# Second-level sums of W_down: one DRAM copy summed in place, and a third set formed on VectorE

## The chip, the cores and the metric

The kernel runs on one core of a Trainium2 chip. The metric is the device time of one execution in microseconds, as the median of several executions. "The profile" is one more execution, recorded by the hardware profiler; its times are counted from the first instruction. TensorE (PE) does the matmuls, VectorE (DVE) and ScalarE (ACT) the element-wise work, GpSimd (POOL) small operations and all DMAs that convert or accumulate, SyncE (SP) issues the other DMAs. All DMAs share 16 DMA engines.

## What is computed

A transformer block on 2048 rows of width D = 1024: layer norm with a modulation from a condition vector, linear attention, and a second half that is a gated MLP with hidden width F = 3584.

```python
h = _layernorm(x) * (1 + ca) + sa
x = x + ga * _A_ref(h, A_wqkv, A_wo)          # linear attention with its projections
h = _layernorm(x) * (1 + cb) + sb
x = x + gb * ((_gelu(h @ w_gate) * (h @ w_up)) @ w_down)
```

Only the last product, with `w_down` (3584 x 1024), is concerned by the change: not the product itself but the preparation of its weights.

## The kernel before

**Products with sums.** Nearly all matrix products are done in Strassen-Winograd form: seven products of half size instead of eight, at the price of sums of blocks of both operands. Some are nested: one of the seven products is itself done in seven. The sums of activations are made on VectorE. Sums of weights are needed too, and for `W_down` they are made ahead of time and kept in DRAM.

**W_down.** Its 28 row blocks of 128 are split into two interleaved halves (`wd_v[0]`, `wd_v[1]`, 14 blocks each), its columns into two halves of 512, which gives four blocks b11, b12, b21, b22. First-level sums t0 to t3 (f16) lie in the DRAM buffer `ts` (`t_scr`): t0 and t2 are made by DMA alone, as a copy that converts from bf16 and then a transfer that accumulates onto it (`wd_todo`, 28 transfers of 256 KB), t1 and t3 on VectorE in `wd_sums` (line 1080): for each of seven pairs of row blocks it loads the raw rows of the second half and the rows of t0, makes two sums and stores them.

Three of the seven products of the down stage are nested (`NESTED`: b21, b22, t0). Each needs second-level sums of its own weight block. With quarters q11, q12, q21, q22 (even or odd row block, left or right 256 columns) these are q11+q12, q11+q12+q22, q12+q22 and q11+q12+q22+q21. They lie in the DRAM buffer `us` (`u_scr`), one slot for each of three blocks and four sums. `second_sums` (line 1064) writes them as chains of DMAs on GpSimd's queue, each of 448 KB in rows of 512 bytes: for every block two copies, an accumulation onto each, a copy of the first sum, an accumulation, a copy of that, an accumulation. That is 24 transfers, 12 copies and 12 accumulations; 8 of the copies are between buffers of the same type or within `us`.

**The order of the work.** All instructions are recorded first and then ordered by a planner (`Plan`). The order on TensorE is the order of recording; on the other engines the planner puts ready instructions by due times, which it finds by sweeping forward and backward over the program with a price for each instruction. A DMA's price is its bytes (`op.bytes`) at 360 GB/s in one serial pipe, plus a latency; an accumulating DMA counts three times its bytes. The result is a fixed order for every engine; at run time an engine waits only for data and for buffers to come free.

`paced_moves` (line 1049) ties a group of DMAs on GpSimd to the progress of the work: a one-element GpSimd copy (L1052) reads a tile that the work has just produced, and the DMAs (issued at L1035) follow it. The 24 transfers are paced so: four after the transformed rows of block 1 (near 48 us), four after those of block 3 (near 117 us), and the other sixteen in the gate/up stage of the first half of the rows: units n = 1 to 4 take two transfers each (second-level sums of b21 and b22), units 5 to 12 one each (those of t0).

**The gate/up stage** (`gate_up`, 248 to 425 us for the first half, 505 to 671 for the second) runs 14 units of some 12 us. Each unit loads 1 MB of `w_gate` or `w_up` (`w_unit`, L1325) into one of three buffers, so that the load of unit n+2 goes out when unit n-1 has ended; VectorE makes the block sums of the next unit's weight (L550, the line of the helper `tt_op`), as fillers between its other work. In the first half, every second unit also runs `wd_sums` for one pair of row blocks and moves two first-level pieces. The norm of the second half of the rows (`late_norm`) also runs here and uses GpSimd for a power (L1204) and for stores (L1208).

**The down stage** (`down_out`, 425 to 505 and 671 to 756 us) reads the sums: `nested` loads seven quarters for each nested product on SP's queue (L1604), four of them second-level sums.

Of the kernel before, what the change touches and what calls it, by code (L numbers as in the profile page):

```python
# [10 lines left out]
FP32 = mybir.dt.float32  # L11
BF16 = mybir.dt.bfloat16
F16 = mybir.dt.float16
AF = mybir.ActivationFunctionType
ALU = mybir.AluOpType
# [8 lines left out]
class Plan:  # L24
# [101 lines left out]
    def aim(self, op):  # L126

        self.ops[-1].early.add(op.n)
        op.late.add(len(self.ops) - 1)

    def cost(self, op, outs, ins):

        size = lambda a: math.prod(d[1] for d in a.ap[1:])
        n = max(size(a) for a in (outs if op.eng == "PE" else outs + ins))
        psum = any(a.tensor.name.startswith("psum") for a in outs + ins)
        wide = any(a.dtype == FP32 and size(a) > 8 for a in outs + ins)
        ptrs = sum(size(a) == 1 for a in ins)
        if op.eng == "PE":
            op.cost = n / 2.4 + 2.5
            op.lat = op.cost + 165  # L140
            if op.fn == "matmul" and outs[0].ap[0][1] <= 32:
                op.cost /= 3.5
        elif op.fn.startswith("dma"):
            a = outs[0]
            op.cost, op.bytes = 1000 if op.eng == "POOL" else 450, math.prod(d[1] for d in a.ap) * (4 if a.dtype == FP32 else 2)
            op.bytes *= 3 if "accum_op" in op.kw else 1
            op.load = a.tensor.name.startswith("mem")
            if op.fn == "dma_start_transpose":
                op.cost, op.bytes = self.transpose
            op.lat = op.cost  # L150
        elif op.eng == "ACT":
            op.cost = (55 if psum else 112) + n / 1.2 + 85 * ptrs
            op.lat = op.cost + 115
            f = op.kw.get("func")
            op.table = "g" if f == AF.Gelu_apprx_tanh else "e" if f in (AF.Exp, AF.Ln) else None
        elif op.eng == "POOL":
            op.cost = 500 if n <= 8 else 250 + n / 0.46
            op.lat = 1800 if n <= 8 else op.cost
        else:
            rate = 1.0  # L160
            if op.fn in ("tensor_scalar", "tensor_scalar_mul", "tensor_scalar_add", "tensor_copy") and not wide:
                rate = 1.0 if psum else 4.0
            elif op.fn == "tensor_tensor" and not wide:
                rate = 2.0
            op.cost = 69 + n / (0.96 * rate) + 61 * ptrs
            op.lat = op.cost + 83
# [119 lines left out]
def kernel(  # L286
# [14 lines left out]
    P = 128  # L301
# [4 lines left out]
    S, D = x_in.shape  # L306
    F = B_w_gate.shape[1]
    KD = D // P
# [6 lines left out]
    NW = min(TG, D)  # L315
# [11 lines left out]
    NPR = JF // 2  # L327
# [4 lines left out]
    mem = mem_pool.tile([P, 103 * KB + KB // 2], BF16, name="mem", tag="mem")  # L332
# [51 lines left out]
    def at(off, shape, dt):  # L384
        return Ring(off, shape, dt, 1)()
# [44 lines left out]
    HB = TG // 2  # L430
# [16 lines left out]
    hr1 = [h12[b // 2][:, b % 2] for b in range(4)]  # L447
# [49 lines left out]
    wdr_ring = Ring(189, [2, D], BF16, 1)  # L497
    wds_ring = Ring(193, [2, 2, NW], F16, 1)
    wds_ring.slots += Ring(183, [2, 2, NW], F16, 1).slots
    wdt_ring = Ring(197, [2, NW], F16, 1)  # L500
    sub_a = [at(76 + 3.5 * j, [NPR // 2, HB], F16) for j in range(3)]
    sub_b = [at(189 + 3.5 * j, [NPR // 2, HB], F16) for j in range(4)]
    x2_ring = Ring(191, [D], BF16, 4)
# [17 lines left out]
    scr_pool = ctx.enter_context(tc.tile_pool(name="scr", bufs=1, space=bass.MemoryType.DRAM))  # L521
# [3 lines left out]
    den_scr = [scr_pool.tile([2, P // DH, 2, KH * TG], BF16, name=f"den{pr}", tag=f"den{pr}") for pr in range(2)]  # L525
    x2_scr = [scr_pool.tile([TG, D], BF16, name=f"x2s{b}", tag=f"x2s{b}") for b in range(NG)]
    t_scr = scr_pool.tile([P, 4, NPR, NW], F16, name="ts", tag="ts")
    u_scr = scr_pool.tile([P, NPR // 2, 3, 4, HB], F16, name="us", tag="us")

    nc.scalar.add_instruction(  # L530
        mybir.InstLoadActFuncSet(name=nc.get_next_instruction_name(), ins=[], outs=[],
# [4 lines left out]
    te, ve, ac, gp, sy = (plan.on(e) for e in ("PE", "DVE", "ACT", "POOL", "SP"))  # L536
# [12 lines left out]
    def tt_op(out, a, b, op):  # L549
        ve.tensor_tensor(out=out, in0=a, in1=b, op=op)  # L550
# [207 lines left out]
    def ln1_block(b):  # L758
        plan.ahead = 4000 if b > 1 else 14000
        for tl in range(TT):  # L760
            xt = load_x(b * TT + tl)
            if b == 1:
                plan.chain.insert((1, 2, 5, 7)[tl], plan.ops[-1])
            mv = ln_stats(xt)
            rstd = pool_rstd(mv)
            nb = nb_ring()
            gp.tensor_scalar(out=nb, in0=mv[:, 0:1], scalar1=rstd, scalar2=-1.0, op0=ALU.mult, op1=ALU.mult)
            xh = xh_ring()
            ac.activation(out=xh, in_=xt, func=AF.Identity, scale=rstd, bias=nb)
            gp.dma_start(out=xa_scr[b][tl * P:(tl + 1) * P, :], in_=xh)  # L770
        sy.dma_start_transpose(out=hr1[b], in_=xa_scr[b][:])
        if b == NG - 1:
            wd_moves(hr1[b][:, 0, 0:1], NPR)
        for kd in range(KD):
            ve.tensor_scalar(out=hr1[b][:, kd, :], in0=hr1[b][:, kd, :], scalar1=opcA[:, kd:kd + 1],
                             scalar2=modT[:, kd:kd + 1], op0=ALU.mult, op1=ALU.add)
        if b != 2:
            paced_moves(hr1[b][:, KD - 1, 0:1], two[b - 1] + two[b])
        plan.ahead = 14000

    def h_sum(b, j):
# [250 lines left out]
    wd_v = B_w_down.rearrange("(i fh p) n -> fh p i n", fh=2, p=P)  # L1032

    def move(dst, src, add):
# [3 lines left out]
    wd_full = {"b11": wd_q[0, 0], "b12": wd_q[0, 1], "b21": wd_q[1, 0], "b22": wd_q[1, 1],  # L1038
               **{f"t{j}": t_scr[:, j] for j in range(4)}}
    NESTED = ("b21", "b22", "t0")  # L1040

    def wd_quarter(name, kh, h):
        return wd_full[name].rearrange("p (i e) n -> e p i n", e=2)[kh][:, :, h * HB:(h + 1) * HB]
# [5 lines left out]
    def paced_moves(seen_of, moves):  # L1049

        plan.hold([op for op in plan.ops if op.eng == "PE"][-1])
        gp.tensor_copy(out=seen, in_=seen_of)  # L1052
        plan.hold(plan.ops[-1])
        for dst, src, add in moves:
            move(dst, src, add)
        plan.hold()
# [4 lines left out]
            paced_moves(seen_of, wd_todo[:n])  # L1061
            del wd_todo[:n]

    def second_sums():


        def chain(x, o):
            q11, q12, q21, q22 = (x[:, :, e, h, :] for e in range(2) for h in range(2))
            o0, o1, o2, o3 = (o[:, :, f, :] for f in range(4))
            return [(o0, q11, 0), (o2, q12, 0), (o0, q12, 1), (o2, q22, 1), (o1, o0, 0), (o1, q22, 1), (o3, o1, 0), (o3, q21, 1)]  # L1070

        raw = wd_v[1].rearrange("p (c e) (j h n) -> p c e j h n", e=2, j=2, h=2)
        t0 = wd_full["t0"].rearrange("p (c e) (h n) -> p c e h n", e=2, h=2)
        b21, b22 = (chain(raw[:, :, :, j], u_scr[:, :, j]) for j in range(2))
        return [[b21[i], b22[i]] for i in range(8)], chain(t0, u_scr[:, :, 2])

    two, t_chain = second_sums()
    late_moves = [two[4], two[5], two[6], two[7], *([m] for m in t_chain)]

    def wd_sums(c):  # L1080


        raw, t, tt = wdr_ring(), wdt_ring(), wds_ring()
        rows = slice(2 * c, 2 * c + 2)
        plan.ahead, plan.extra = 60000, 6000
        sy.dma_start(out=raw, in_=wd_v[1][:, rows, :])
        sy.dma_start(out=t, in_=wd_full["t0"][:, rows, :])
        plan.ahead, plan.extra = 14000, 0

        def last():  # L1090
            tt_op(tt[:, 1], tt[:, 0], raw[:, :, 0:NW], ALU.add)
            for j in range(2):
                gp.dma_start(out=wd_full[f"t{2 * j + 1}"][:, rows, :], in_=tt[:, j])

        return [lambda: tt_op(tt[:, 0], t, raw[:, :, NW:D], ALU.add), last]

    def kvq_phase():

# [301 lines left out]
    def gate_up(g):  # L1400
        h = h2
        rows_inner(g)
        late = late_norm(g + 1) if g + 1 < NGR else []
        w = w_unit(g, 0)
# [19 lines left out]
        inner = None  # L1424
        for n in range(NU):
# [47 lines left out]
            if g == 0 and n % 2 == 0:  # L1473
                fill += wd_sums(n // 2)
                wd_moves(w["s1"][:, 0, 0, 0:1], 2)
            if g == 0 and 1 <= n <= len(late_moves):
                paced_moves(w["s1"][:, 0, 0, 0:1], late_moves[n - 1])
            five = Inner(Y, w["inner"]["t1"], h_inner[g, "t1"]) if "t1" in w["inner"] else None
            if five:
                five.s15()  # L1480
# [28 lines left out]
            inner = None  # L1509
# [23 lines left out]
            w = w_next  # L1533
# [8 lines left out]
    def down_out(g):  # L1542
        NC = 2
        last = g == NGR - 1
# [48 lines left out]
        def nested(name, A, S, keep, out):  # L1593


            j, x = NESTED.index(name), A.rearrange("p (k e) t -> p e k t", e=2)
            at_w = W_AT[g][name]
            dt = F16 if name[0] == "t" else BF16
            y11, y21, y22 = (quarters(at_w[n], [NPR // 2, HB], dt) for n in (0, 1, 6))
            t1, t0, t2, t3 = (quarters(at_w[n], [NPR // 2, HB], F16) for n in (2, 3, 4, 5))  # L1600
            for t, src in ((y11, wd_quarter(name, 0, 0)), (y21, wd_quarter(name, 1, 0)), (t1, u_scr[:, :, j, 1, :]),
                           (t0, u_scr[:, :, j, 0, :]), (t2, u_scr[:, :, j, 2, :]), (t3, u_scr[:, :, j, 3, :]),
                           (y22, wd_quarter(name, 1, 1))):
                sy.dma_start(out=t, in_=src)  # L1604
            x11, x12, x21, x22 = (x[:, e, :, h * HB:(h + 1) * HB] for h in range(2) for e in range(2))
# [123 lines left out]
        def run(*steps):  # L1729
            for f in steps:  # L1730
                f()
# [70 lines left out]
```

## Time and profile before

| | us |
|---|---|
| median of 8 executions | 755.98 |
| lowest and highest | 754.29, 757.92 |
| the profiled execution | 757.47 |
| its span from first to last instruction | 755.7 |
| mean granted clock of TensorE | 0.995 |

The DMA traffic on the two queues, and the transfers that belong to the sums of W_down (line or buffers, engine that issues, number, size of each, median us from issue to landing):

```profile
q1 hardware_dynamic: 128832, 122.44, 53.8%
q0 software_dynamic: 26592, 29.37, 18.2%
...
mem<-us SPq DMA_DIRECT2D x24, 448.0 KB, 8.3
mem<-ts SPq DMA_DIRECT2D x6, 1792.0 KB, 8.5
...
ts<-in_B_w_down_dram POOLq DMA_DIRECT2D x28, 256.0 KB, 8.7
us<-in_B_w_down_dram POOLq DMA_DIRECT2D x12, 448.0 KB, 9.7
```

q1 carries the DMAs of SyncE, q0 those of GpSimd; the columns are packets, MB and the time that the packets took as a share of 16 engines over the span. `mem` is the on-chip memory, `us` and `ts` are the two DRAM buffers. The 12 transfers of the last line are those that read the raw weight; six more go from `us` to `us` and six from `ts` to `us`.

### The profile page before, as it was taken

The page shows a single profiled execution, that of the slowest core. Times are in us where ns is not written, and L with a number is a line of the kernel's source. Part 1 is how long each engine was busy: PE and PEld are TensorE (multiplying, and loading weights), DVE is VectorE, ACT ScalarE, POOL GpSimd, SP SyncE. Part 2 cuts the span into 40 slices and gives each one's busy share as a digit, 9 for nine tenths or more (in the row PEclk, how much of TensorE's full clock was granted, in tenths as well). Part 3 has the DMA queues.
Part 4 walks back from the last instruction along what each step waited for, and adds up shares of the span by engine and source line. Part 5 has one row for each costly group of instructions (what it writes and reads, how often), then busy time and mean ns, then how long its engine had stood idle before and what let it go on. Part 6 is the DMA issues. An engine that isn't in the chain of part 4 may idle for free.

```text
span 755.7 us, 11423 instructions
## 1 busy us (share of the span) xinstructions
PE 731.3 (97%) x4150; PEld 389.4 (52%) x4164; DVE 585.0 (77%) x1230; ACT 432.6 (57%) x757; POOL 120.1 (16%) x183
## 2 busy tenths in 40 slices
PE   5999899999999997999999999999999999999997
PEld 2444445444444443444555486645555555548664
DVE  7897987577775974868797689658788889887763
ACT  3674476669762656989876316017777777641000
POOL 2351257000000240543432000010000000000000
PEclk9999999999999998999999999999999999999999
DMA  9888379939899987998987979952322313399822
GB/s 313 313 179 175 122 172 164 316 137 290 221 295 246 350 184 241 237 319 234 245 228 139 281 227 279 320 182 85 112 75 93 112 57 112 100 273 296 285 99 74
DMA packets 157832, 154.62 MB, mean 205 GB/s; under 512 B 34000, under 2 KB 135888, under 8 KB 156496
## 3 DMA queue, kind: packets, MB, share of 16 engines
q1 hardware_dynamic: 128832, 122.44, 53.8%
q0 software_dynamic: 26592, 29.37, 18.2%
q10 hardware_dynamic: 2352, 2.10, 0.8%
q8 instruction: 32, 0.52, 0.3%
q14 instruction: 24, 0.20, 0.1%
HBM read 127.01 MB, written 37.88 MB: 218 GB/s over the span
## 4 chain that ended last, share of the span: by engine, by line
PE 78%; DMA 9%; DVE 6%; ACT 3%; issue 2%; POOL 1%; SPq 1%; DVEq 0%; ACTq 0%; POOLq 0%
PE psum L1364 30%; PE psum L1570 13%; PE psum L1614 8%; PE psum L1375 7%; PE psum L1244 6%; PE psum L856 5%; PE psum L926 5%; DVE mem L550 4%; DMA mem<-in_B_w_up_dram 2%; DMA mem<-in_B_w_gate_dram 2%; DMA mem<-in_A_wqkv_dram 2%; DMA mem<-in_w_mod_dram 1%; DMA mem<-xas 1%; PE psum L955 1%; DMA xas<-mem 1%
## 5 line engine op out<-in xcount | busy, mean ns | idle before, releaser
L550 DVE TENSOR_TENSOR mem<-mem 128x1024 f16<-128x1024 bf16 (+11 forms) x641 | 303.1, 515 | 41.5 <-ACT mem L801 19.2
L1364 PE MATMUL psum<-mem 128*128 128x512 f16 x1248 | 301.8, 381 | 4.7 <-DVE mem L550 3.1
L801 ACT ACTIVATE mem<-psum 128x256 f32<-128x256 f32 (+3 forms) x284 | 154.3, 562 | 117.4 <-PE psum L1364 42.2
L550 DVE TENSOR_TENSOR mem<-psum,mem 128x512 f16<-128x512 f32 (+4 forms) x204 | 154.8, 766 | 67.0 <-ACT mem L801 21.9
L1364 PEld LDWEIGHTS <-mem 128*128 128x128 f16 (+1 forms) x1248 | 122.7, 98 | 117.4 <-issue 8.8
L1570 PE MATMUL psum<-mem 128*128 128x512 f16 (+2 forms) x458 | 99.0, 372 | 0.7 <-DVE mem L550 0.5
L1375 PE MATMUL psum<-mem 128*128 128x256 f16 x560 | 90.0, 273 | 2.2 <-DVE psum L550 1.9
L1375 PEld LDWEIGHTS <-mem 128*128 128x128 f16 (+1 forms) x560 | 54.9, 98 | 47.9 <-issue 6.3
L1570 PEld LDWEIGHTS <-mem 128*128 128x128 f16 x462 | 45.2, 98 | 49.8 <-issue 0.7
L1614 PE MATMUL psum<-mem 128*128 128x256 f16 (+1 forms) x588 | 66.2, 273 | 0.0
L856 PE MATMUL psum<-mem 128*128 128x512 f16 (+1 forms) x272 | 61.8, 379 | 1.2 <-DVE mem L550 0.8
L1614 PEld LDWEIGHTS <-mem 128*128 128x128 f16 x588 | 57.5, 98 | 9.2
L1418 ACT ACTIVATE psum<-psum 128x512 f32<-128x512 f32 x56 | 32.9, 587 | 44.2 <-PE psum L1364 28.9
L1244 PE MATMUL psum<-mem 128*128 128x512 f16 x256 | 56.0, 379 | 0.0
L926 PE MATMUL psum<-mem 128*128 128x512 f16 x224 | 51.2, 379 | 0.0
L550 DVE TENSOR_TENSOR psum<-psum,mem 128x256 f32<-128x256 f32 x80 | 34.3, 428 | 14.5 <-ACT mem L801 13.8
L856 PEld LDWEIGHTS <-mem 128*128 128x128 f16 x280 | 27.1, 98 | 32.2 <-issue 1.1
L1244 PEld LDWEIGHTS <-mem 128*128 128x128 bf16 x256 | 24.8, 98 | 30.4 <-issue 0.4
L1435 ACT ACTIVATE mem<-psum 128x512 f16<-128x512 f32 x56 | 33.0, 595 | 10.2 <-PE psum L1364 10.1
L1445 ACT ACTIVATE mem<-mem 128x512 f16<-128x512 f16 x56 | 34.1, 625 | 5.3 <-DVE mem L550 5.0
L926 PEld LDWEIGHTS <-mem 128*128 128x128 f16 (+1 forms) x224 | 21.6, 98 | 27.0 <-issue 2.0
L1035 POOL DMA_DIRECT2D ts<-in_B_w_down_dram x28 | 35.3, 1614 | 0.8 <-DMA ts<-in_B_w_down_dram 0.7
(132 smaller groups left out, 556.0 us busy)
## 6 DMA issues: line engine op xcount, KB each, us to landing
mem<-in_B_w_gate_dram SPq DMA_DIRECT2D x14, 1024.0 KB, 9.3
mem<-in_B_w_up_dram SPq DMA_DIRECT2D x14, 1024.0 KB, 7.5
mem<-in_w_mod_dram SPq DMA_DIRECT2D x24, 512.0 KB, 8.6
mem<-us SPq DMA_DIRECT2D x24, 448.0 KB, 8.3
mem<-ts SPq DMA_DIRECT2D x6, 1792.0 KB, 8.5
mem<-in_A_x_dram SPq DMA_DIRECT2D x32, 256.0 KB, 7.4
ts<-in_B_w_down_dram POOLq DMA_DIRECT2D x28, 256.0 KB, 8.7
us<-in_B_w_down_dram POOLq DMA_DIRECT2D x12, 448.0 KB, 9.7
```

The source lines that it names most:

```text
L550: ve.tensor_tensor(out=out, in0=a, in1=b, op=op)
L801: ac.activation(out=t, in_=ps, func=AF.Copy)
L856: te.matmul(ps, lhsT=A[:, k, i * P:(i + 1) * P], rhs=B[:, k, :], start=(start and k == 0), stop=(k == KH - 1), skip_group_check=True)
L926: te.matmul(o, lhsT=W[:, k, (j0 + i) * P:(j0 + i + 1) * P], rhs=h_form(a, k), start=(start and k == 0), stop=(k == KH - 1), skip_group_che ...
L1035: gp.dma_start(out=dst, in_=src, **(dict(accum_op=ALU.add) if add else {}))
L1244: te.matmul(psw[:, half, :], lhsT=pqT[b][:, g, tl * P:(tl + 1) * P], rhs=Wp[:, g, half * NW:(half + 1) * NW], start=(g == 0), stop=(g == K ...
L1364: te.matmul(ps, lhsT=a[:, k, e, :], rhs=b[:, k, :], start=(start and k == 0), stop=(k == KH - 1), skip_group_check=True)
L1375: te.matmul(ps, lhsT=self.x[a][:, k, :], rhs=self.y[y][:, k, :], start=(start and k == 0), stop=(k == KH // 2 - 1), skip_group_check=True)
L1435: ac.activation(out=o, in_=ps, func=AF.Gelu_apprx_tanh)
L1445: ac.activation(out=o, in_=o, func=AF.Gelu_apprx_tanh)
L1570: te.matmul(psm[:, q, c], lhsT=A[:, i, q * P:(q + 1) * P], rhs=wt[:, i, c], start=(start and i == 0), stop=(i == NPR - 1), skip_group_chec ...
L1614: te.matmul(ps[:, q, :], lhsT=a[:, k, q * P:(q + 1) * P], rhs=y[:, k, :], start=(start and q == 0 and k == 0), stop=(k == NPR // 2 - 1), s ...
```

## The change

The buffer `us` is replaced by two.

- `ub` holds one f16 copy of the whole second row half of W_down (both blocks b21 and b22 with all their quarters). It is written by two copying transfers (`sums_copy`, even and odd row blocks, 1.75 MB each, rows of 2048 bytes) and then summed in place by four accumulating transfers (`sums_add`, 896 KB each), each of which serves both blocks: q12 is added onto q11, q22 onto q12, the new q11 onto q22, the new q22 onto q21. The four quarters then hold the four sums. The first copy goes where four transfers were in block 1, the first accumulation where four were in block 3; the second copy is in unit 1 of the gate/up stage, the other accumulations in units 3, 5 and 7.
- `ut` holds the second-level sums of t0. They are made on VectorE in `wd_sums`, from the rows of t0 that it holds anyway: four sums of 128x256 for each of seven chunks, and one store of 256 KB on GpSimd's queue. They have two new small on-chip buffers.
- `nested` reads its four sums through `second_sum`, which picks the place in `ub` or `ut`.
- The planner's price for DMAs from DRAM to DRAM is changed: it now depends on the length of contiguous runs and on whether the transfer accumulates.

```diff
@@ Plan.cost
+    def run(self, ap):
+        n = 1
+        for stride, size in reversed(ap.ap):
+            if stride != n or (ap.tensor.name.startswith("mem") and (stride, size) == tuple(ap.ap[0])):
+                break
+            n *= size
+        return min(n * (4 if ap.dtype == FP32 else 2), 4096)
...
-            op.bytes *= 3 if "accum_op" in op.kw else 1
+            run = min(self.run(a) for a in outs + ins)
+            if not any(a.tensor.name.startswith("mem") for a in outs + ins):
+                op.bytes = int(op.bytes * self.GBPS * (12 + run / 27) / 16 / run * (2.3 if "accum_op" in op.kw else 1.6))
@@ buffers
+    wdu_ring = Ring(187, [4, HB], F16, 1)
+    wdu_ring.slots += Ring(199, [4, HB], F16, 1).slots
...
-    u_scr = scr_pool.tile([P, NPR // 2, 3, 4, HB], F16, name="us", tag="us")
+    ub_scr = scr_pool.tile([P, 2, NPR // 2, D], F16, name="ub", tag="ub")
+    ut_scr = scr_pool.tile([P, NPR // 2, 4, HB], F16, name="ut", tag="ut")
@@ ln1_block
-            paced_moves(hr1[b][:, KD - 1, 0:1], two[b - 1] + two[b])
+            paced_moves(hr1[b][:, KD - 1, 0:1], sums_copy[0:1] if b == 1 else sums_add[0:1])
@@ second_sums is removed
-    late_moves = [two[4], two[5], two[6], two[7], *([m] for m in t_chain)]
+    sum_q = ub_scr.rearrange("p e c (j s n) -> p e c j s n", j=2, s=2)
+    sums_copy = [(ub_scr[:, e], wd_v[1].rearrange("p (c e) n -> p e c n", e=2)[:, e], 0) for e in range(2)]
+    flat = ub_scr.rearrange("p e c (j s n) -> p e (c j) s n", j=2, s=2)
+    sums_add = [(flat[:, e, :, s, :], flat[:, f, :, t, :], 1)
+                for e, s, f, t in ((0, 0, 0, 1), (0, 1, 1, 1), (1, 1, 0, 0), (1, 0, 1, 1))]
+    late_moves = {1: sums_copy[1:2], 3: sums_add[1:2], 5: sums_add[2:3], 7: sums_add[3:4]}
+
+    def second_sum(name, f):
+        if name == "t0":
+            return ut_scr[:, :, f, :]
+        e, h = ((0, 0), (1, 1), (0, 1), (1, 0))[f]
+        return sum_q[:, e, :, NESTED.index(name), h, :]
@@ wd_sums
-        raw, t, tt = wdr_ring(), wdt_ring(), wds_ring()
+        raw, t, tt, ut = wdr_ring(), wdt_ring(), wds_ring(), wdu_ring()
...
-        return [lambda: tt_op(tt[:, 0], t, raw[:, :, NW:D], ALU.add), last]
+        def inner():
+            q11, q12, q21, q22 = (t[:, e, h * HB:(h + 1) * HB] for e in range(2) for h in range(2))
+            for out, a, b in ((0, q11, q12), (2, q12, q22), (1, ut[:, 0], q22), (3, ut[:, 1], q21)):
+                tt_op(ut[:, out], a, b, ALU.add)
+            gp.dma_start(out=ut_scr[:, c], in_=ut)
+
+        return [lambda: tt_op(tt[:, 0], t, raw[:, :, NW:D], ALU.add), last, inner]
@@ gate_up
-            if g == 0 and 1 <= n <= len(late_moves):
-                paced_moves(w["s1"][:, 0, 0, 0:1], late_moves[n - 1])
+            if g == 0 and n in late_moves:
+                paced_moves(w["s1"][:, 0, 0, 0:1], late_moves[n])
@@ nested
-            for t, src in ((y11, wd_quarter(name, 0, 0)), (y21, wd_quarter(name, 1, 0)), (t1, u_scr[:, :, j, 1, :]),
-                           (t0, u_scr[:, :, j, 0, :]), (t2, u_scr[:, :, j, 2, :]), (t3, u_scr[:, :, j, 3, :]),
+            for t, src in ((y11, wd_quarter(name, 0, 0)), (y21, wd_quarter(name, 1, 0)), (t1, second_sum(name, 1)),
+                           (t0, second_sum(name, 0)), (t2, second_sum(name, 2)), (t3, second_sum(name, 3)),
```

## The prediction

> **What bounds the kernel now.** I read the busy table first, then TensorE by stage, then TensorE's waits, and then the chain of waits back from the longest one.
>
> ```profile
> PE 731.3 (97%) x4150; PEld 389.4 (52%) x4164; DVE 585.0 (77%) x1230; ACT 432.6 (57%) x757; POOL 120.1 (16%) x183
> ```
>
> TensorE is busy for 97% of the 755.7 us span. The change takes no matmul away and adds none, so all it can give or take are the 24 us in which TensorE idles, and time in which TensorE runs at half clock. Busy time by stage (columns: window, length, busy us of PE, PEld, DVE, ACT and POOL, granted clock, DMA share, GB/s):
>
> ```profile
> 0.00:28.00 28.00, 18.06 (x120) 8.44 (x120) 20.93 (x69) 11.64 (x23) 8.04 (x32) 1.00 0.96 333
> 28.00:88.00 60.00, 57.39 (x324) 27.66 (x327) 52.66 (x124) 33.39 (x50) 17.69 (x29) 1.00 0.74 191
> 248.00:425.00 177.00, 170.65 (x861) 84.94 (x860) 134.18 (x297) 132.58 (x249) 58.80 (x76) 0.98 0.89 245
> 505.00:671.00 166.00, 165.48 (x950) 92.75 (x949) 140.50 (x344) 120.84 (x249) 1.43 (x2) 1.00 0.35 106
> ```
>
> The first 28 us (10 idle) and the end (4.4 idle after 671 us) are not touched. The rest that this change can reach is in two rows: 2.6 us idle between 28 and 88 us, and 6.35 us idle in the first gate/up stage (248 to 425 us), the only row whose clock is below 1.00 and the one with a nearly full DMA. The second gate/up stage, with hardly any DRAM-to-DRAM traffic, idles 0.5 us. The waits of TensorE and of VectorE that matter (engine and line, whom it waited for, us in total, times, longest), then the chain of waits at that place (start us, us, what):
>
> ```profile
> PE psum L1364 <- DVE mem L550: 3.1, 1, 3.1
> DVE mem L550 <- DMA mem<-in_B_w_gate_dram: 6.9, 1, 6.9
> ```
>
> ```profile
> 272.14 13.19 DMA mem<-in_B_w_gate_dram
> 285.33 0.02 issue
> 285.36 1.71 DVE mem L550 x4
> ```
>
> One weight load, issued at 272.14, took 13.19 us (median of its kind 9.3). VectorE, which works in a fixed order, stood 6.9 us before the sums of that weight, and TensorE 3.1 us behind VectorE. The same windows in steps of 5 us show what it cost and what the DMA did before:
>
> ```profile
> 260.00:265.00 5.00, 3.95 (x21) 1.86 (x19) 4.09 (x11) 2.71 (x7) 0.00 (x0) 1.00 0.85 284
> 265.00:270.00 5.00, 4.96 (x25) 2.44 (x25) 4.68 (x11) 3.25 (x6) 1.51 (x4) 1.00 0.40 125
> ...
> 280.00:285.00 5.00, 4.00 (x23) 2.10 (x22) 0.00 (x0) 1.47 (x3) 0.74 (x1) 1.00 1.21 274
> 285.00:290.00 5.00, 2.03 (x8) 0.94 (x8) 4.56 (x11) 2.92 (x6) 0.73 (x1) 0.81 1.17 371
> 290.00:295.00 5.00, 5.00 (x15) 1.91 (x13) 2.33 (x5) 2.51 (x6) 0.57 (x1) 0.51 1.01 375
> ```
>
> After the wait the granted clock is 0.81 and then 0.51: 15 matmuls fill five us that hold 25 to 29 elsewhere. In the timeline of TensorE this unit's block of 24 matmuls starts at 276.06 and the next at 295.14, 19.1 us, where regular units take 11.9 (307.29 to 319.17). **This one stall costs 7.2 us.** The Trainium skill (TensorE: Matmul & The Clock Gate, Part 1) ties the half clock to a whole idle window of some 3.4 us. The gap here is 3.1 us and the clock fell all the same, so by the rule removing the stall gives 3.1 + 0.9 = 4.0 us (0.9: VectorE's second wait at 289), by the row 7.2. I take the row.
>
> What stood in the load's way is in GpSimd's timeline (start us, us, instruction, [idle before]):
>
> ```profile
> 255.45 1.49 POOL L1035 DMA_DIRECT2D us<-us  x2
> ...
> 270.12 3.08 POOL L1035 DMA_DIRECT2D us<-in_B_w_down_dram  x2 [0.80 <-issue]
> 271.66 3.03 POOL L1035 DMA_DIRECT2D ts<-in_B_w_down_dram  x2
> ```
>
> Two accumulating transfers of second-level sums go out 2 us before the load, two first-level moves with it.
>
> **The price of the transfers.** By the packet records of the software queue, a 512-byte packet takes 41 to 50 ns where it casts, some 68 ns where it accumulates; a 1024-byte one 59 and 102; a 4096-byte one (same-type copies, stores from SBUF) 160. A 448 KB transfer is 896 rows of 512 bytes, 56 on each of 16 engines: 2.6 us of all engines as a casting copy, 3.8 accumulating, 1.1 as same-type copy. Removed: 4 casting copies, 12 accumulating, 8 same-type copies: 10 + 46 + 9 = 65 us. Added: two copies of 1.75 MB, 896 rows of 2048 bytes each. No row shows that size: the step from 512 to 1024 bytes (18 ns) carried on gives 95 ns, twice the 1024-byte row 118, so 5.3 to 6.6 us each; I take 6. Four accumulating transfers of 1792 rows: 7.6 us each, 30. Seven 256 KB stores of sums from SBUF: 0.6 us each, 4. Together 46 us, so 19 us of DMA time go, 12 of them before 140 us. Reads of the sums in the down stage keep their number, size and 512-byte rows.
>
> **Part by part, where it lies.**
> 1. *Unit 2 (270 us).* Its pair of accumulating transfers goes: 7.6 us of DMA, of which by the packet records some 1300 of 1792 packets (5.5 us) ran within the load's flight. The load lands at 278 to 280 instead of 285.3; VectorE gets there at 278.4. VectorE's wait of 6.9 us turned into 3.1 us of TensorE's, so it has 3.8 us of cover; 0 to 1.5 us vanish in it. Gain 7.2 us. Next in line there is unit 5's load (item 3).
> 2. *Unit 1 (255 us).* In place of two same-type copies (2.2 us) comes one 1.75 MB copy: 3.1 to 4.4 us more DMA, in a stretch that is full (shares 1.07 and 0.99 from 250 to 260). Up to 270 us the rows above leave (0.15 + 0.60) x 5 = 3.75 us. So it just fits. But ScalarE waits 1.8 us at 263.9 for the last store of x2 rows and TensorE then idles 1.09 us. The Trainium skill (DMA: Bandwidth & Descriptors, Queues, rings and completion order) says that an engine takes its rings in turn; a turn of 95 to 118 ns against 51 ns (the hardware queue's 1024-byte packet) would cut weight loads to a third while the copy lasts, where 512-byte rows left them half. It speaks against this part: by it the store comes up to 4.4 us later and TensorE idles up to 5.5; by the spare time in the rows, nearly nothing. I take 1.5 us loss, nearer the rows, since most of the copy is through when that store is issued (258.96).
> 3. *Units 3, 5, 7.* One 896 KB accumulating transfer each (7.6 us), where units 2, 4 and 5 to 12 had 448 KB pieces. The one of unit 3 goes out near 280 us and meets unit 5's load (issued at 284). Nothing if that load stays under some 13 us (the second late load, 14.7 us, cost 0.8); the whole 7.2 if it becomes the next stall. Taken at 0.
> 4. *28 to 88 us.* Four copies (10 us of DMA, 3.7 us of GpSimd) between the rstd steps of the next block and its stores become one of 6 us and some 1.6 us. That chain (GpSimd 47.7, stores to 65, transpose to 74, sums to 86) ends in waits of 0.73, 0.71 and 0.84 us. Gain 0 to 2.3; I take 1.
> 5. *106 to 140 us.* Four accumulating transfers become one: 7.6 us less DMA. TensorE idles 0.2 us from 88 to 137, so 0.
> 6. *VectorE.* 28 sums of 128x256 f16, 283 ns in the row of that shape: 7.9 us, where VectorE is idle 43 of 177 us. Cover gone, they would cost at most 7.9. Each stands behind sums that already wait for the same rows: no new wait. 0.
> 7. *GpSimd.* 18 fewer moves and 7 more stores of 0.6 to 0.8 us; its waits for its own transfers (12.4 us) shrink. Each new store waits for four sums of VectorE; behind it are first-level moves and the pow of the next half's norm, needed at 505 us. SP's queue gets nothing new before its first read of these sums at 404. 0.
> 8. *The planner's prices.* They move orders on every engine but TensorE. Its DRAM-to-DRAM total falls from 102 to 91 us at its own rate, first-level copies rise 1.75-fold. Bound: minus 1 to plus 6 us (one stall like item 1's made elsewhere); taken at 0.
>
> Sum against the profiled execution: 757.5 - 7.2 + 1.5 - 1.0 = 750.8 us. The median is 1.5 us below that execution; whether its stall is shorter I can't see, so I count 1.2 of it as such: 756.0 - 5.5 = **750.5 us**.
>
> **Rivals.**
> *Forecast, 50%:* the stall goes, small ones come: 745.5 to 754.
> *The stall moves, 20%:* the larger accumulating transfer of unit 3 delays unit 5's load (7.5 us + 7.6 us = 15 us), and 5 to 7 us come back: 753.5 to 757, taken at 755.5. For it: two loads of 13 to 15 us exist already. Against: the load of 14.7 us cost 0.8 us, and DMA time falls.
> *Slower, 30%:* the big copy at 255 us. Place: last x2 store and unit 3's load; price: TensorE's wait of 1.09 us grows by 3 to 4.4 us, past the length at which the clock fell, with 3.3 us of half clock, and the backlog reaches the load of 272 us, so that its stall stays. 756 + 6.5 = 762.5, from 758 on. It decides once a 2048-byte packet takes over 120 ns, as 3.75 us of spare time are then used up. For it: the full rows. Against: the copy starts 3.5 us before that store.
> That the transfers don't do less DMA work is excluded by their row counts unless accumulating packets grow; 5 ns more a packet adds 2.2 us in all, hidden.
>
> **Chances and range.** The runs shown spread over 3.6 us; 0.2% (1.5 us) is what can be told from no change. Faster: the forecast and a fifth of the second case, 0.53. Within: the rest of it but a bit, 0.13. Slower: 0.34. Range 745.5 (all of items 1 and 4, one more us) to 762; the likeliest case's own is 745.5 to 754.
>
> **What would show it.** Right: no wait of TensorE over 2 us and granted clock 1.00 in 248 to 425 us, the load of unit 4 under 10 us, software queue near 1900 engine-us (18.2% of the span to 16%). Wrong: a clock of 0.5 anywhere after 28 us; ScalarE waiting over 4 us for x2 stores near 264; casting packets of 2048 bytes over 120 ns; VectorE waiting for unit 5's load.

## The result, and the profile after

| | before | after |
|---|---|---|
| median, us | 755.89 (32 runs) | 748.75 (11 runs) |
| lowest to highest | 753.79 to 761.73 | 747.89 to 750.97 |
| ratio, with its 95% interval | | 0.9908 (0.9891 to 0.9925) |
| profiled execution, and its span | 757.47, 755.7 | 748.54, 746.4 |

The change saves 7.1 us. The forecast was 750.5, its range 745.5 to 762.

The busy table of the changed kernel and its software queue:

```profile
PE 729.4 (98%) x4150; PEld 388.6 (52%) x4164; DVE 589.5 (79%) x1258; ACT 432.8 (58%) x757; POOL 96.2 (13%) x164
...
q0 software_dynamic: 20592, 27.53, 15.7%
```

GpSimd is 24 us less busy and its queue fell from 18.2% to 15.7% of 16 engines, near the 16% of the forecast. VectorE has the 28 new sums. TensorE by stage (columns as before):

```profile
28.00:88.00 60.00, 59.66 (x334) 28.58 (x337) 53.82 (x128) 35.09 (x51) 14.77 (x31) 1.00 0.64 193
...
248.00:425.00 177.00, 175.69 (x898) 87.81 (x898) 145.17 (x335) 133.11 (x250) 44.98 (x63) 1.00 0.88 247
...
505.00:671.00 166.00, 165.06 (x936) 91.45 (x936) 139.39 (x331) 115.90 (x239) 0.20 (x1) 1.00 0.38 114
```

Both rows that could give something gave it: TensorE idles 0.3 us from 28 to 88 (2.6 before), and 1.3 in the window that held 6.35 us of idling and a clock of 0.98. TensorE's three longest waits (us in total, times, longest):

```profile
PE psum L676 <- DVE mem L663: 5.3, 1, 5.3
PE psum L713 <- DMA mem<-in_c_dram: 2.3, 1, 2.3
PE psum L1393 <- DVE psum L564: 1.2, 4, 0.4
```

The first two are in the first 10 us and were there before; after 28 us no single wait is longer than 0.5 us. GpSimd's timeline at the place of the old stall, and unit 4's weight load in the list of DMA issues (KB, us to landing):

```profile
253.28 0.98 POOL L1049 DMA_DIRECT2D ub<-in_B_w_down_dram  x1
...
267.27 1.43 POOL L1049 DMA_DIRECT2D ts<-in_B_w_down_dram  x2
...
283.36 2.02 POOL L1049 DMA_DIRECT2D ub<-ub  x1
```

```profile
mem<-in_B_w_gate_dram SPq DMA_DIRECT2D x1, 1024.0 KB, 8.1
```

Unit 2 has only its first-level moves now, and unit 4's weight load (issued at 268.77) lands after 8.1 us instead of 13.2. Where the 9.3 us of span went is read from TensorE's timeline, from the first matmul of each stage to that of the next. The same was read in the profiled execution of every run below:

| us, profiled execution | start to output projection | output projection | gate/up, first half | down | gate/up, second half | down |
|---|---|---|---|---|---|---|
| before | 187.87 | 59.71 | 177.46 | 80.44 | 165.47 | 84.75 |
| after | 185.69 | 59.71 | 169.35 | 80.44 | 166.43 | 84.78 |
| unit 2 light | 188.07 | 59.71 | 169.80 | 80.44 | 165.47 | 84.81 |
| early copies at 94 us | 190.99 | 59.71 | 177.12 | 80.44 | 165.48 | 84.76 |
| these two together | 192.77 | 59.71 | 171.30 | 80.44 | 165.48 | 84.80 |
| new prices only | 186.27 | 58.82 | 173.83 | 80.44 | 164.85 | 84.79 |
| old prices | 186.27 | 63.70 | 173.14 | 80.44 | 165.39 | 84.76 |
| two adds back | 185.21 | 59.71 | 169.18 | 80.44 | 166.44 | 84.72 |
| copy twice | 186.38 | 59.71 | 177.70 | 80.44 | 166.44 | 84.73 |
| copy in 512-byte rows | 185.23 | 59.72 | 171.96 | 80.44 | 166.43 | 84.72 |
| early copies at 105 us, unit 2 light | 186.24 | 59.72 | 170.35 | 80.44 | 165.44 | 84.81 |
| early copies at 105 us, units 2 to 4 shifted | 186.58 | 59.71 | 173.46 | 80.44 | 165.45 | 84.76 |
| prices 1.7 and 2.4 | 187.21 | 58.91 | 172.99 | 80.44 | 166.31 | 84.74 |
| new sums twice | 186.35 | 59.72 | 173.49 | 80.44 | 166.42 | 84.78 |

Before to after: 2.2 us at the start and 8.1 in the first gate/up stage are gained, 1.0 in the second is lost. One profiled execution can lie off its median: that of the kernel before is 1.6 us above its own, those of "old prices" and "these two together" are 2.1 and 3.3 above theirs, that of "units 2 to 4 shifted" is 2.5 below. The first column scatters too: five runs with the changed kernel's order (after, two adds back, copy twice, copy in 512-byte rows, new sums twice) start the output projection between 185.21 and 186.38, though the early copy is the same in all of them. The last but one column doesn't: 165.44 to 165.48 in the six runs with the order of before, 166.42 to 166.44 in these five.

### The profile page after: what moved, and what is told of

It is laid out like the page before. It is cut to its first block, busy times and chain, and to the rows that moved or that the text cites. A ratio compares the mean times of both kernels' runs of the same rounds, so it can differ in the third digit from the quotient of the medians.

```text
span 746.4 us, 11425 instructions
## 1 busy us (share of the span) xinstructions
PE 729.4 (98%) x4150; PEld 388.6 (52%) x4164; DVE 589.5 (79%) x1258; ACT 432.8 (58%) x757; POOL 96.2 (13%) x164
## 3 DMA queue, kind: packets, MB, share of 16 engines
q0 software_dynamic: 20592, 27.53, 15.7%
## 4 chain that ended last, share of the span: by engine, by line
PE 84%; DVE 5%; ACT 5%; DMA 3%; issue 2%; SPq 1%; ACTq 0%; DVEq 0%
PE psum L1382 30%; PE psum L1588 13%; PE psum L1632 9%; PE psum L870 8%; PE psum L1393 7%; PE psum L1262 7%; PE psum L940 5%; DVE mem L564 5%; PE psum L969 4%; DMA mem<-in_A_wqkv_dram 2%; DMA mem<-in_w_mod_dram 1%; PE psum L984 1%; ACT mem L815 1%; DVE psum L564 1%; ACT psum L1436 1%
## 5 line engine op out<-in xcount | busy, mean ns | idle before, releaser
L564 DVE TENSOR_TENSOR mem<-mem 128x512 f16<-128x512 f16 (+8 forms) x669 | 307.3, 505 | 25.6 <-ACT mem L815 10.8
L1049 POOL DMA_DIRECT2D ts<-in_B_w_down_dram x28 | 28.4, 1197 | 9.0 <-DMA ts<-in_B_w_down_dram 8.4
```

## The experiments

The difficulty is that the change does two things at once: it changes transfers, and by that and by the prices it makes the planner put every engine but TensorE in another order. Most of the runs therefore keep one fixed order and alter a transfer only when it is issued. Medians are set against 755.2 to 755.5 us of the kernel before, which ran beside them, and against 748.75 of the changed kernel, which did not: the kernel before read 755.89 beside that one. Differences to 748.75 of less than 1 us therefore mean nothing. The diffs show the main lines of each edit, with comments that stand only here.

### Unit 2's transfers made light, order of before

```diff
+                if n == 2:
+                    for op in plan.ops[-2:]:   # issued so, planned as before
+                        plan.instead[op.n] = [dict(op.kw, out=op.kw["out"][:, 0:1], in_=op.kw["in_"][:, 0:1])]
```

> The kernel before with the same instruction order on every engine; only the two accumulating transfers of unit 2 (L1035, 270 us) move one row block of seven, so that the rest of these two second-level sums is left out. Theory (traffic): these two transfers held up unit 4's weight load. It lands in 8 to 10 us instead of 13.2, VectorE's wait of 6.9 us falls below 2, TensorE's 3.1 us wait and the half clock go, and the time falls by 7.2 us to 748.7 (747.5 to 750). Rival (order): the fixed order put the weight sums too early on VectorE, whatever the traffic; TensorE still waits over 2 us near 284 us, time 754.5 to 756.

749.56 us, ratio 0.9924 (0.9900 to 0.9949). From the list of DMA issues near 270 us (KB, us to landing), and VectorE's waits:

```profile
mem<-in_B_w_gate_dram SPq DMA_DIRECT2D x1, 1024.0 KB, 8.8
us<-in_B_w_down_dram POOLq DMA_DIRECT2D x2, 64.0 KB, 4.9
```

```profile
DVE mem L551 <- DMA mem<-in_B_w_gate_dram: 2.5, 1, 2.5
```

The load went from 13.2 to 8.8 us, VectorE's wait from 6.9 to 2.5 (a little more than the 2 expected), TensorE has no wait between 262 and 300 us, and the stage of the profiled execution is 7.7 us shorter with all orders unchanged. By the medians the gain is 6.0 us (755.51 to 749.56). The profiled execution of before also has the wait of 1.09 us at 264 us, ahead of these transfers, and this one has not; against the run "early copies at 94 us", which has the stall but not that wait, the stage is 7.3 us shorter. In the kernel before, the two transfers made the stall.

### The same two transfers put back into the changed kernel

```diff
+                if n == 2:
+                    op = plan.ops[-2]
+                    raw = wd_v[1].rearrange("p (c e) n -> p e c n", e=2)[:, 1]
+                    plan.instead[op.n] = [dict(out=no_scr[:, :, j * HB:(j + 1) * HB],
+                                               in_=raw[:, :, j * NW + HB:(j + 1) * NW], accum_op=ALU.add)
+                                          for j in range(2)] + [op.kw]
```

`no_scr` is a buffer that nobody reads; the copy that fills it, after block 3, is left out here.

> The changed kernel with its own order on every engine, and with two accumulating transfers of 448 KB put back in unit 2, ahead of its first-level moves, into a buffer that nobody reads (it is filled by one more copy after block 3). Theory (traffic alone sets the stall): unit 4's load grows from 8.1 to 13 us, VectorE stands before its sums, TensorE waits over 2 us near 280 us, time 754 to 757. Rival (the new order gives cover: VectorE now comes to these sums 9 to 12 us after the load's issue, where it came 6.3 us after it before): the load grows as much, TensorE waits under 1 us, time 748.5 to 751.

749.02 us, ratio to before 0.9930 (0.9910 to 0.9949): nothing is lost that these runs could tell. The issues of that stretch, and VectorE's timeline:

```profile
mem<-in_B_w_gate_dram SPq DMA_DIRECT2D x1, 1024.0 KB, 12.9
no<-in_B_w_down_dram POOLq DMA_DIRECT2D x2, 448.0 KB, 13.9
```

```profile
282.04 0.68 DVE L566 TENSOR_TENSOR mem<-mem 128x1024 f16<-128x1024 bf16 x1
```

The load is as slow as in the kernel before, but VectorE's first sum of it comes at 282.04, 13.8 us after its issue at 268.26 and so after its landing. In the old order VectorE came to it 6.3 us after the issue. So the stall has two remedies, lighter traffic or a later place on VectorE, and the changed kernel has both; each alone suffices. The rival's reading was right here.

### The prices alone, and the changed transfers with the old prices

The first is the kernel before with the new rule in `Plan.cost`, the second the changed kernel with

```diff
-            run = min(self.run(a) for a in outs + ins)
-            if not any(a.tensor.name.startswith("mem") for a in outs + ins):
-                op.bytes = int(...)
+            op.bytes *= 3 if "accum_op" in op.kw else 1
```

> The kernel before with the planner's new prices and the old transfers. Theory (the transfers carry the gain): a new order with the old traffic, 753 to 760, and a load of a weight over 12 us with a TensorE wait over 1 us in the first gate/up stage. Rival (the prices carry it, since the planner now puts the weight sums where the loads really land): 747 to 750.5 with no such wait.

> The changed kernel with the planner's old prices. Theory (the transfers carry the gain): 748 to 751.5, no granted clock below 0.9 in the first gate/up stage. Rival (the prices carry it): 754 or more, with a stall of over 2 us there.

Prices alone: 751.85 us, ratio 0.9964 (0.9951 to 0.9976), just below the band of the one theory and above that of the other. Old prices: 753.69 us, ratio 0.9994 (0.9975 to 1.0013), no difference from before that is clear of noise, and between the bands of both theories. Its 14 executions fall in two groups, eight from 751.3 to 753.9 us and six from 755.8 to 757.8, and the profiled one is of the upper group. Neither half has the stall at 284 us any more. Each has another one, by TensorE's waits, the first line from the prices alone, the second from the old prices:

```profile
PE psum L1375 <- DVE mem L561: 3.9, 1, 3.9
```

```profile
PE psum L1260 <- DVE mem L562: 3.0, 1, 3.0
```

The one is at 247 us, at the start of the gate/up stage, where its chain of waits runs through six sums of VectorE. The other is at 210 us in the output projection; the chain of waits before it:

```profile
186.36 10.79 DMA mem<-den
...
205.22 6.25 DMA xhs<-mem
```

Loads of the attention's denominators and a store of normed rows, then VectorE. No transfer that the change touches stands in either chain: I take these as stalls of the order, which no run tested.

### Other prices

The changed kernel with 1.7 and 2.4 for 1.6 and 2.3.

> The changed kernel with its two price factors a little higher (1.7 and 2.4 for 1.6 and 2.3): same transfers, another order. It shows how much of the result is the luck of one order. Theory (the order counts as much as the transfers): differs from the changed kernel by 1 us or more, 747 to 755. Rival (with right prices any order does): within 0.8 us of it, 748 to 749.6.

753.39 us, ratio to before 0.9985 (0.9969 to 1.0000). The transfers are the same and most of the gain is gone; ScalarE's wait at 267 us:

```profile
ACT mem L815 <- DMA x2s<-mem: 4.7, 1, 4.7
```

Its store of x2 rows took 9.7 us in the chain of waits, beside the big copy; TensorE waited 2.8 us. This is one of the signs by which the prediction would have been wrong (ScalarE waiting over 4 us for x2 stores near 264): with the same copy, but in another order, it came. Three orders for the changed transfers give 748.75, 753.69 and 753.39 us, two orders for the old ones 755.5 and 751.85.

### The copy of unit 1: twice, and in short rows

```diff
+                if n == 1:      # twice
+                    plan.instead[op.n] = [op.kw, dict(op.kw, out=no_scr[:, 0])]
+                if n == 1:      # in the other run: rows of 512 bytes
+                    plan.instead[op.n] = [dict(op.kw, out=op.kw["out"][:, :, c], in_=op.kw["in_"][:, :, c]) for c in q]
```

> The changed kernel, same order, with the 1.75 MB copy of unit 1 sent twice, the second time into a buffer that nobody reads. It tests how near the slower case of the prediction was. Theory (the copy just fits in the spare DMA time before 270 us): 5.5 us more of all engines spill over, ScalarE waits for the last x2 store or VectorE for a load, TensorE gains waits of 2 us or more, time 751 to 757. Rival (the cover is much larger): within 1 us of the changed kernel, 748 to 749.7.

> The changed kernel, same order, with the 1.75 MB copy of unit 1 cut into four of 448 KB with rows of 512 bytes. By the packet times, 3584 packets of 41 to 50 ns, 9 to 11 us of all engines instead of 6. Theory (DMA time counts): as much as 60 per cent of the effect of the doubled copy, up to 752. Rival (packet size counts: weight loads and x2 stores get a larger share beside short packets): unit 3's load gets shorter than with long rows, and the time is 748 to 749.

Twice: 757.28 us, 8.5 us slower than the changed kernel. In its chain of waits and its 5 us windows:

```profile
257.90 15.93 DMA mem<-in_B_w_up_dram
```

```profile
270.00:275.00 5.00, 0.62 (x3) 0.20 (x2) 1.15 (x4) 0.84 (x2) 0.37 (x1) 0.89 1.10 394
275.00:280.00 5.00, 5.00 (x15) 1.90 (x14) 4.66 (x11) 0.96 (x2) 0.00 (x0) 0.50 0.97 314
```

Unit 3's load, next to the copies, takes 15.9 us, VectorE stands before its sums, TensorE idles 4.4 us and then runs at half clock. This is the slower case of the prediction, at its place; one copy is short of it by less than the length of a second one.

Short rows: 751.91 us, 3.2 us slower than the changed kernel, with the same bytes. ScalarE's timeline at the x2 store, in this run and then in the changed kernel, and VectorE's wait in this run:

```profile
264.09 2.07 ACT L816 ACTIVATE mem<-psum 128x512 f16<-128x512 f32 x4 [2.14 <-DMA x2s<-mem]
```

```profile
263.49 1.57 ACT L815 ACTIVATE mem<-psum 128x512 f16<-128x512 f32 x3 [1.09 <-DMA x2s<-mem]
```

```profile
DVE mem L565 <- DMA mem<-in_B_w_up_dram: 1.5, 1, 1.5
```

Unit 3's load took 12.0 us in the chain of waits, and VectorE waits 1.5 us for it; in the changed kernel VectorE waits for no weight load in this stage. ScalarE's wait for the x2 store is 1.09 us there and 2.14 here, but it says less: with the new sums twice, whose transfers are those of the changed kernel, it is 2.19. The short rows take 10.2 us of all engines (3584 packets of 45.7 ns on the mean) against 6.7 for the long ones. So the longer DMA time outweighed whatever the smaller packets gave back; how much that is, this run can't tell, since both changed at once.

### The early copies, put off

Two tries, both with the order of before otherwise. In the first the four copies of block 1 go out after block 3's stores, alone and with unit 2 light; in the second with the first-level moves of 105 us, with unit 2 light.

```diff
+            if b == 1:
+                early.extend(plan.ops[-4:])
+                plan.instead.update({op.n: [] for op in early})
+            plan.before[first.n] = early   # first: the pacing copy, or the first move after it
```

> The kernel before with the same order on every engine but for one thing: the four copies of block 1 (GpSimd, 47 to 58 us) are issued only after the stores of block 3 (near 97 us). Theory: they delayed block 2's chain (rstd, stores, transpose) by their issue and their traffic; TensorE's waits of 0.73, 0.71 and 0.84 us at 77, 81 and 86 us go, TensorE reaches the first matmuls of the output projection at 185.7 instead of 187.9, time 753.7. Rival: that gain came from a new order of the planner; the waits stay within 0.5 us in sum and the time is 755.9.

> Both edits of the two runs before it (four copies of block 1 later, unit 2's two accumulating transfers at one row block of seven, the rest of these two sums left out), same order otherwise. Theory: the two gains add up, 755.9 - 7.2 - 2.2 = 746.5, below the changed kernel (748.75), because that one lost 1.0 us in the second gate/up stage by its new order. Rival: the gains are one and the same slack or another stall comes next: 748.5 to 752.

> The kernel before, same order; the four copies of block 1 are issued with the first-level moves at 105 us, after the transpose of block 3 has landed (in the earlier try they met that transpose, which took 15.8 us instead of some 8, and TensorE waited 4.5 us for it), and unit 2's two accumulating transfers move one row block of seven, the rest of these two sums left out. Theory: TensorE starts the output projection at 185.7 instead of 187.9 and the first gate/up stage takes 169.8 instead of 177.5 us; in all 746.5 (745.5 to 748). Rival (wherever these copies go they delay something of the attention phase): the start stays at 187 or later, time 749 to 752.

The first try is slower: 760.29 us, ratio 1.0061 (1.0039 to 1.0082); with unit 2 light 752.94, ratio 0.9968 (0.9955 to 0.9981). Both expectations were missed. The windows of the run alone, and its chain of waits:

```profile
28.00:88.00 60.00, 59.68 (x338) 29.03 (x341) 56.40 (x133) 36.43 (x53) 16.35 (x32) 1.00 0.52 163
88.00:137.00 49.00, 44.34 (x221) 20.74 (x223) 33.92 (x58) 29.36 (x33) 27.64 (x32) 0.97 1.03 167
```

```profile
96.13 15.83 DMA mem<-xas
```

Up to 88 us the theory holds: TensorE idles 0.3 us instead of 2.6. But at the new place the copies meet block 3's transpose, which takes 15.8 us; in the kernel before it takes 6.0 (issued at 99.48, GpSimd goes on at 105.44), not the 8 of the last expectation, which is nearer GpSimd's wait for it (8.3). TensorE then waits 4.5 us and loses clock. At 105 us, with the transpose landed, the gain stays: 748.42 us, ratio 0.9907 (0.9888 to 0.9927), start at 186.24, gate/up stage 170.35; the median lies just above the 745.5 to 748 expected. Of the 2.2 us hoped for at the start 1.6 came; a wait of 0.83 us for a `w_mod` load at 156 us is new. This is the changed kernel's time in the old order and with the old prices, with part of two sums left out.

### Timing instead of less traffic

The early copies at 105 us; the transfers of units 2 to 4 one unit later each, nothing left out.

```diff
+                if 2 <= n <= 5:
+                    now = plan.ops[-len(late_moves[n - 1]):]
+                    plan.before[now[0].n] = held[:]
+                    held[:] = now if n < 5 else []
...
```

> The kernel before with all its transfers and sums and the same order but for GpSimd's: the four copies of block 1 at 105 us as in the run beside this one, and the transfers of units 2, 3 and 4 one unit later each. It asks whether the load of unit 4 can be cleared by timing alone. Theory: unit 4's load lands within 10 us, the accumulating transfers meet unit 5's load (issued 12 us later) instead; if VectorE's place for that one gives the same 6 us, the stall moves there: 752 to 756. Rival (only unit 4 is tight): no stall, 746 to 748.5.

754.66 us, ratio 1.0004 (0.9985 to 1.0022). A stall came, but not at the load that was expected. The chain of waits, and TensorE's timeline:

```profile
317.92 14.07 DMA mem<-in_B_w_gate_dram
```

```profile
334.10 0.41 PE L1385 MATMUL psum<-mem 128*128 128x256 f16 x2 [3.21 <-DVE psum L553]
```

Unit 4 is clear, and unit 5 too; a load issued at 317.9 us is held up instead, that of unit 8. Which transfers held it up was not tested. With the old order and full traffic there is a stall still, at another place.

### The new sums twice

```diff
                 tt_op(ut[:, out], a, b, ALU.add)
+                plan.instead[plan.ops[-1].n] = [plan.ops[-1].kw] * 2
```

> The changed kernel, same order, with each of the 28 new sums of VectorE issued twice, 7.9 us more of VectorE in the first gate/up stage. Theory (they lie in VectorE's idle time): within 0.5 us of the changed kernel. Rival (VectorE has no room left there): 1 to 8 us slower.

751.41 us, 2.7 us slower than the changed kernel, against less than 0.5 expected. TensorE's waits:

```profile
PE psum L1395 <- DVE psum L565: 3.6, 8, 1.0
```

Eight short waits, where the changed kernel has four of 1.2 us in sum. Part of the time may not be due to the sums: TensorE also waits 0.97 us behind the x2 store here, as it does with the short rows (0.92), and doesn't in the profiled execution of the changed kernel. VectorE's 32 us of idling in that stage are not all free room at the places where the sums stand.

## Why the prediction was right

The time, the sign and the two places were right; the shares of the causes were not. With the old order held, lighter traffic in unit 2 and the early copies put off give as much as the change (748.42 us, with part of two sums left out). The change as made, however, came with a new order, which the prediction took at nothing, and in two other orders the same transfers give 753.69 and 753.39. That this order met the forecast is in part luck.

1. **Unit 2: right in its place and near its size, too narrow in its cause.** 7.2 us were forecast; with the order held, 7.3 to 7.7 came in the profiled executions and 6.0 by the medians. By the half-clock rule that the prediction cites it would have been 4.0. In the changed kernel, however, the order alone also covers that load. (By the trace 1744, not some 1300, of the two transfers' 1792 packets started in the load's flight, and after 671 us TensorE idles 4.1 us within the span, not 4.4; nothing rests on either.)
2. **Unit 1: right in the balance, over-charged by 1.5 us.** The copy fits: ScalarE still waits for the x2 store, 1.09 us, but TensorE doesn't wait behind it. A 2048-byte packet takes 98 ns at the median and 119 on the mean, 6.7 us for a copy, against 6 taken, and just under the 120 from which the prediction let the slower case decide. That it was near the edge is shown by the doubled copy, and by the order with the prices 1.7 and 2.4, in which the same copy made ScalarE wait 4.7 us. By the rule on taking turns that the prediction cites, long rows are the worse neighbours while they last; here the short rows, which last longer, were the slower.
3. **Units 3, 5, 7: right.** Nothing new waits. That a stall can come at another load is shown by the shifted run, in the old order.
4. **28 to 88 us: mis-sized, 1 taken and 2.2 measured,** within the bound of 2.3; by the scatter of the starts it can be 1.5 to 2.9. The four copies were the cause in the old order (idle 2.6 to 0.3 us when they go). The prices alone, with the four copies left in block 1, also start at 186.27, so here too there are two remedies.
5. **106 to 140 us: right;** TensorE is busy for 48.79 of 49 us from 88 to 137.
6. **VectorE: 0 taken, not fully free.** With a second set of 28 sums the kernel is 2.7 us slower; what the first costs was not measured.
7. **GpSimd: right;** it waits for none of its own second-level transfers.
8. **The planner's prices: the term that failed.** It was taken at 0 with a bound of minus 1 to plus 6 us. Prices alone take 3.7 us off by the medians (2.7 by the ratio), more than the bound allows; without them the changed transfers lose 4.9 of their 7.1 (3.8 if only the lower group of executions is counted). On the other side the new order costs 1.0 us in the second gate/up stage, which keeps that length with two adds back, the copy twice or the sums twice; it adds up in steps of at most 0.4 us, and why was not traced.

Against the profiled execution 6.7 us were forecast, and 9.3 us of span came: 2.4 more in the first gate/up stage (item 2's 1.5, and smaller waits that went too; the 1.09 us behind the x2 store is missing in other runs of the old order as well, so its going may be chance), 1.2 more at the start, 1.0 less in the second gate/up stage. By the medians it is 7.1 instead of 5.5. The 1.5 us between the profiled execution of before and its median, which the prediction could not explain, fit the half clock: 40 of the 103 executions of the kernel before beside the experiments have a granted clock of 0.995, as the profiled one, and a median of 756.1 us; 60 have 0.997 or 0.998, and 754.5.

Shown, then: the load's delay by the two transfers, the stall's price, the early copies' price, and that one order more or less is worth as much as the transfers. By medians and at equal prices, the transfers give 1.7 us at the old prices (755.4 to 753.7; by the ratio 0.5, which is not clear of noise) and 3.1 at the new (751.85 to 748.75). Open: how the transfers would fare over many orders; five orders are few.

## What to carry to other kernels

Where a planner makes the order, test a change of traffic with the order held fixed, by altering the transfer at issue: only then is its effect apart from the luck of a new order. A stall behind a late load has two remedies, less traffic before it or a later place of its first reader, and a profile shows which of them is near: the reader's distance from the load's issue (6.3 us here) against the load's time (8 to 13 us). Before a transfer is moved, look for what it meets at its new place; a transpose that grew from 6.0 to 15.8 us cost more than the move had saved.

## What the runs showed of the hardware

**Half clock goes by stretches of 3.41 us.** Within a run, all changes of the clock record lie a whole number of 3.413 us apart, and a half-clock stretch after 28 us is 3.41 or 6.83 us long (the last of a record, cut off by its end, is left out). I cut the 14 profiled executions along that grid, from 28 to 735 us. Of the stretches at full clock, eight held 2.27 us or more of TensorE's idling (by the matmul ends that the trace gives), and all eight were followed by half clock; no other held over 1.65 us, and none of those was. So a gap's place on the grid counts beside its length. The gap of 3.10 us (before) had 2.42 us in one stretch, and the clock fell; that of 2.79 us (prices 1.7 and 2.4) was split into 1.65 and 1.14, and it did not. The half clock lasted two stretches where the first of them still held 0.86 us of idling or more (0.86 in the kernel before), and one where it held 0.67 or less. At half the clock a busy stretch loses half its time, so a gap of 3 us costs 3 us, 4.7 or 6.4. Near the start less idling was enough: two profiled executions (unit 2 light, prices 1.7 and 2.4) went to half clock at 15.5 and 15.3 us, after stretches with 1.56 and 1.37 us of it.

**Same-type copies are packed.** Copies between f16 buffers with 512-byte rows appear as packets of 4096 bytes (159 ns at the median), while converting and accumulating ones keep their rows: 512 bytes 41 ns converting and 65 accumulating, 1024 bytes 60 and 102, 2048 bytes 98 converting (medians; on the mean, beside other traffic, 119 for the last).
